# A maximum over partitions by two products of TensorE, placed behind the values, in a decode kernel with attention and a gated feed-forward

## The chip, the core and the metric

The kernel runs on one core of a Trainium2 chip. A core has five engines that run side by side and wait for each other by semaphores: TensorE (PE in the profile; its loads of the stationary operand are listed as PEld), VectorE (DVE), ScalarE (ACT), GpSimd (POOL) and SyncE (SP), which issues most of the transfers. The transfers themselves are done by 16 DMA engines, which bring data from HBM to the on-chip memory SBUF. TensorE writes its results to PSUM, a second on-chip memory in banks of 512 values per partition. The metric is the device time of one execution in microseconds (us).

## What is computed

One token is decoded. `g * attention(x) + (1 - g) * feed_forward(x)`, with `g` a sigmoid of a product of `x` and `gate_w`.

```python
# B, Sq, D = 1, 1, 512;  Hq, Hkv, Sk, Dh = 32, 8, 32768, 128;  F = 1792;  all float32
def _A_ref(x, k_cache, v_cache, wq, wo):
    q = (x @ wq).reshape(B, Sq, Hq, Dh).transpose(0, 2, 1, 3)
    k = jnp.repeat(k_cache, rep, axis=1)          # rep = 4 query heads on each head of the cache
    v = jnp.repeat(v_cache, rep, axis=1)
    scores = jnp.einsum("bhqd,bhkd->bhqk", q, k) * (Dh ** -0.5)
    p = softmax(scores, axis=-1)
    o = jnp.einsum("bhqk,bhkd->bhqd", p, v)
    return o.transpose(0, 2, 1, 3).reshape(B, Sq, Hq * Dh) @ wo

def _B_ref(x, w1, w3, w2):
    return (silu(x @ w1) * (x @ w3)) @ w2

g = sigmoid((x * gate_w).sum(-1, keepdims=True))
return g * _A_ref(...) + (1 - g) * _B_ref(...)
```

The caches of keys and of values are 134 MB each, and every byte is read once. The softmax needs, for each of the 32 query heads, the largest of 32768 scores before the exponentials.

## The kernel before

**Units.** The eight heads of the cache are taken in pairs. A pair's keys come in four units of 8 MB, so there are 16 units of keys (`t` = 0 to 15), and its values in four units of 8 MB (`v`). Values run `LAG` = 4 units behind keys: unit `v` of values is multiplied in the pass of unit `t = v + 4` of keys. Units of keys alternate with units of values in the queue of SP. Two large buffers, `big_a` and `big_b`, take them: keys go to `big_a` (the units 0 and 2 to `big_b`), values to `big_b`. A buffer is loaded again once what reads it is done.

**One pass.** When a unit of keys has landed, ACT sets part of its second half aside (`set_aside`, L318), and DVE transposes it in eight steps (`scores`, L346), two halves `z` of four `c`. Each step gives PE its operand for the scores (L330), added up in one PSUM bank. ACT copies the scores out (L358) and later copies the weights of the values (`weights`, L420, written to `pv`). PE multiplies the unit of values (`values_all`, L432), 32 products, and then a product with zeros (L242) clears the bank of the scores. The next load of keys waits for L318 and for the scores of the second half; the next load of values (L413) waits for L432.

**The softmax.** After each fourth unit (`t` = 3, 7, 11, 15) PE turns the scores of the pair by 16 transpositions into four PSUM banks named `turned` (`turn`, L368), so that 128 positions lie on the partitions and each partition holds 2048 values: 256 positions by 8 heads. DVE then takes the maximum over the 256 (L379, tile `mt`, 128 partitions by 8 heads). The maximum over the 128 partitions follows in eleven small instructions of DVE: a transposition of 32 by 32 blocks (L381), four reductions (L383), one more (L385), four copies that spread it (L388) and a second transposition (L390). Then DVE subtracts it in place (L391), ACT takes the exponentials to `probs` (L398), and DVE sums them in a later pass (L405).

**Order.** The order on every engine is written out by hand. A recorder (`Program.add`) works out the waits from what each step reads and writes; `credits` are semaphores that a PE step waits for and takes down again, as PE runs its passes as real loops: one of 4 passes without values, one of 12 with values. In the second loop the turning stands under a counter, so that it runs in each fourth pass, ahead of the values. Each loop's first instruction is laid on a code block's edge. `columns`, `hidden_products` (L463, the two products of the feed-forward with w1 and w3, once, behind unit 3) and everything behind the second loop are straight-line code. L463 writes the PSUM banks `pm[0]` and `pm[1]` (`ps` in the profile) and reads w1 and w3 from `big_b`; the first load of values waits for it.

**The end.** Behind the loop come the last two heads' values (L587), the products with wo (L574, L660) and with w2 (L676), and the store. Transfers of 8 MB, 4 MB and at last 3.5 MB in five pieces bring their operands. The first load into `big_a` behind the loop is multiplied by L587 and is followed there by another load, which waits for it.

## Time and profile before

| what | value |
|---|---|
| median of 3 runs | 694.13 us (693.95 to 694.29) |
| the profiled execution | 693.89 us, its span 692.1 us |
| bytes read from HBM | 296.23 MB, 428 GB/s over the span |
| busy: PE, DVE, ACT | 388.3, 370.1 and 134.7 us |
| share of the 16 DMA engines taken by the loads | 99.1% |
| granted clock of TensorE, mean | 0.802 |

The span goes from the first to the last instruction of the program. The page of the profile gives busy times by engine, a picture of the span in 40 slices, the DMA queues, the chain of work that ended last, and groups of instructions by line. The order of time lists instructions as "start, duration, engine, line, operation, out<-in, count [idle time before it <- what ended it]". A window's row lists the stretch, its length, the busy time and the count of instructions of PE, PEld, DVE, ACT and POOL, the granted clock, the share of the DMA engines and GB/s. The waits of SP are the time in which a load was not yet issued; a load that is issued also queues behind those issued before it.

### The profile page before, as it was taken

What the parts mean: (1) busy time and instruction counts of PE and PEld (TensorE: products, weight loads), DVE (VectorE), ACT (ScalarE), POOL (GpSimd) and SP (SyncE); (2) the same over time, 40 slices, a digit from 0 to 9 for tenths busy, and PEclk for the clock granted to TensorE, in tenths of its full rate; (3) what the DMA queues carried; (4) which work ended last, traced back from release to release, by engine and by line L of the source; (5) the groups of instructions that cost most, each with busy time, mean ns of one, the idle gap of its engine ahead of it and who ended that gap; (6) DMA issues with size and microseconds to landing.
All of it is one profiled execution on the core that took longest, in us unless ns stands there. A gap on an engine that the chain in (4) does not pass through costs nothing. (4 is left out here: it accounts for less than half of the span.)

```text
span 692.1 us, 5789 instructions
## 1 busy us (share of the span) xinstructions
PE 388.3 (56%) x2448; PEld 95.3 (14%) x2448; DVE 370.1 (53%) x259; ACT 134.7 (19%) x113; POOL 2.8 (0%) x15
## 2 busy tenths in 40 slices
PE   1537677566473636565564646364563646564457
PEld 0101111201010101201010101101010101211112
DVE  1049998493725637493826537492816547600701
ACT  0143323222303131220303131220303031100000
POOL 1000000000000000000000000000000000000000
PEclk9969999968686966778695779788697879865789
DMA  9999999999999999999999999999999999999996
GB/s 394 444 432 424 428 424 432 449 439 432 424 432 424 443 447 432 428 428 428 432 443 443 428 428 428 428 443 447 432 424 428 428 436 439 421 451 425 422 429 287
DMA packets 6213, 296.35 MB, mean 428 GB/s; under 512 B 694, under 2 KB 698, under 8 KB 1084
## 3 DMA queue, kind: packets, MB, share of 16 engines
q1 hardware_dynamic: 6196, 296.23, 99.1%
q8 instruction: 6, 0.10, 0.1%
q14 instruction: 3, 0.02, 0.0%
q10 hardware_dynamic: 8, 0.01, 0.0%
HBM read 296.23 MB, written 0.00 MB: 428 GB/s over the span
## 5 line engine op out<-in xcount | busy, mean ns | idle before, releaser
L346 DVE STREAM_TRANSPOSE aside<-big_a 128x2048 f32<-128x2048 f32 x41 | 94.4, 2302 | 184.3 <-DMA big_a<-in_A_k_cache_dram 184.3
L330 PE MATMUL ps<-aside,winc 128*32 128x512 f32 x512 | 89.4, 776 | 168.0 <-PEq L703 167.2
L330 PE MATMUL ps<-kt,winc 128*32 128x512 f32 x512 | 89.0, 772 | 49.1 <-PEq L703 49.1
L318 ACT COPY aside<-big_a 128x6144 f32<-128x6144 f32 x14 | 74.4, 5313 | 171.2 <-DMA big_a<-in_A_k_cache_dram 171.2
L432 PE MATMUL ps<-big_b,pv 128*32 128x512 f32 x768 | 94.9, 650 | 17.4 <-PEq L703 17.4
L346 DVE STREAM_TRANSPOSE kt<-aside 128x2048 f32<-128x2048 f32 x32 | 72.7, 2273 | 0.0
L346 DVE STREAM_TRANSPOSE kt<-big_a 128x2048 f32<-128x2048 f32 x28 | 63.5, 2269 | 0.0
L330 PEld LDWEIGHTS ps<-aside,winc 128*32 128x32 f32 x512 | 13.1, 120 | 236.6 <-issue 236.6
L358 ACT COPY sb<-ps 128x512 f32<-128x512 f32 x16 | 17.1, 1071 | 136.5 <-PE ps L330 136.5
L432 PEld LDWEIGHTS ps<-big_b,pv 128*32 128x32 f32 x768 | 27.7, 119 | 85.0 <-issue 85.0
L346 DVE STREAM_TRANSPOSE aside<-aside 128x2048 f32<-128x2048 f32 x16 | 36.3, 2269 | 0.0
L587 PE MATMUL ps<-big_b,probs 128*32 128x512 f32 x128 | 19.1, 756 | 21.1 <-DMA big_b<-in_A_v_cache_dram 21.1
L330 PEld LDWEIGHTS ps<-kt,winc 128*32 128x32 f32 x512 | 13.1, 120 | 125.4 <-issue 125.4
L596 DVE TENSOR_SCALAR red<-ps,own_b 128x128 f32<-128x128 f32 x2 | 0.7, 350 | 52.7 <-PE ps L587 52.7
L324 ACT COPY winc<-win 128x128 f32<-128x128 f32 x32 | 9.8, 307 | 77.9 <-PE ps L330 77.9
L587 PE MATMUL ps<-big_a,probs 128*32 128x512 f32 x128 | 18.1, 730 | 7.6 <-DMA big_a<-in_A_v_cache_dram 7.6
L346 DVE STREAM_TRANSPOSE aside<-big_b 128x2048 f32<-128x2048 f32 x7 | 16.0, 2291 | 11.0 <-DMA big_b<-in_A_k_cache_dram 11.0
L641 PE MATMUL ps<-win,ones 128*128 128x512 f32 (+1 forms) x40 | 21.8, 631 | 0.0
L242 PE MATMUL ps<-acc 128*128 128x512 f32 x34 | 20.0, 670 | 2.5 <-POOL acc L213 1.5
L379 DVE TENSOR_REDUCE mt<-turned 128x8 f32<-128x2048 f32 x4 | 9.2, 2292 | 20.3 <-PE turned L368 20.3
L405 DVE TENSOR_REDUCE sums<-probs 128x8 f32<-128x2048 f32 x4 | 15.3, 3834 | 2.1 <-ACT probs L398 2.1
L268 PE MATMUL turned<-big_a,xp 128*32 128x512 f32 x64 | 8.6, 699 | 12.0 <-DMA big_a<-in_A_wq_dram 12.0
(94 smaller groups left out, 186.9 us busy)
## 6 DMA issues: line engine op xcount, KB each, us to landing
big_b<-in_A_v_cache_dram SPq DMA_DIRECT2D x2, 4096.0 KB, 25.8
big_b<-in_B_w_dram SPq DMA_DIRECT2D x2, 3584.0 KB, 20.8
aside<-in_A_wo_dram SPq DMA_DIRECT2D x1, 4096.0 KB, 29.4
big_a<-in_A_wo_dram SPq DMA_DIRECT2D x1, 4096.0 KB, 20.4
big_a<-in_B_w_dram SPq DMA_DIRECT2D x2, 1024.0 KB, 23.5
big_a<-in_B_w_dram SPq DMA_DIRECT2D x1, 768.0 KB, 26.0
big_a<-in_B_w_dram SPq DMA_DIRECT2D x1, 512.0 KB, 26.7
big_a<-in_B_w_dram SPq DMA_DIRECT2D x1, 256.0 KB, 26.9
```

The lines of the kernel that those rows point to most:

```text
L242: return T.matmul(ps_s, acc[:, 0:P], acc, start=True, stop=False, skip_group_check=True)
L268: ins = T.matmul(pf[b][32 * j:32 * j + 32, :], xp[:, c, :], t[:, o:o + REP * DH], start=(c == 0), stop=(c == NC - 1),)
L318: act(lambda: A.copy(spare, src[:, :, 32:128]), reads=[key], writes=["wo"])
L324: lambda: A.copy(winc, win[:, t // 4, :, 16 - 16 * z:48 - 16 * z]),
L330: ins = T.matmul(ps_s[32 * g:32 * g + 32, :], winc[:, c, :], kt[c % 2][:, 512 * g:512 * g + 512], start=False, stop=False, skip_group_chec ...
L346: k = dve(lambda d=dst, s=src: V.transpose(d, s), reads=[key], writes=[f"kt{c % 2}"], credit="keys")
L358: lambda: A.copy(sb[:, :, :, t % 4], ps_s.rearrange("p (n i) -> p n i", i=32)),
L379: dve(lambda: V.tensor_reduce(mt[:, 0:8], turned.rearrange("p (n q) -> p q n", q=8), axis=AX.X, op=ALU.max), reads=banks, writes=["mt"])
L405: dve(lambda: V.tensor_reduce(sums[:, 8 * w:8 * w + 8].rearrange("p (u q) -> p u q", u=2), probs[:, :, 0:1024].rearrange("p u (n q) -> p u ...
L432: ins = T.matmul(ps_o[32 * t:32 * t + 32, :], pv[:, o:o + 32], big[1][:, n * P:(n + 4) * P], start=((z, g) == (0, 0)), stop=((z, g) == (1, ...
L587: ins = T.matmul(ps_o[32 * t:32 * t + 32, :], prob[u][:, o:o + 32], vt[:, n * P:(n + 4) * P], start=((e, z, g) == (0, 0, 0)), stop=((e, z, ...
L641: return T.matmul(bank[:, 0:n], ones, win.rearrange("p w c n -> p (w c n)")[:, 0:n], start=True, stop=True)
```

## The change

The maximum over the 128 partitions is done by two products of TensorE. One transposes `mt`, 128 partitions by 8, into 8 partitions by 128 in `pm[0]`; DVE reduces that to `high`, one value on each of 8 partitions, and multiplies the 8 by 8 corner of the unit matrix by it (`diag`). A product of ones (8 by 128) with `diag` then puts all 8 maxima on each of 128 partitions in `pm[1]`, and DVE copies them to `top`. These two products and the steps between them stand right behind the turning in PE's order. In the second loop the turning and the maximum stand behind the values instead of ahead of them; a new semaphore, `maxima`, tells PE when `mt` and when `diag` is written. In unit 3 both products stand ahead of L463. One clearing of `mt` by POOL goes. And DVE's program is preceded by a directive that lays its first instruction on an edge of 128 instructions, with a jump over the padding.

```diff
-    mt, mtt, mark, mark2 = sbuf("mt", 32), sbuf("mtt", 32), sbuf("mark", 1), sbuf("mark2", 1)
-    quads, high, wide_t, top = sbuf("quads", 4), sbuf("high", 1), sbuf("wide_t", 32), sbuf("top", 32)
+    mt, mark, mark2 = sbuf("mt", 8), sbuf("mark", 1), sbuf("mark2", 1)
+    high, diag, top = sbuf("high", 1), sbuf("diag", 8), sbuf("top", 8)
...
+    def maxima(w, loop):
+        banks = [f"f{f}" for f in range(4)]
+        most, spread = pm[0][0:8, 0:P], pm[1][:, 0:8]
+        m = dve(lambda: V.tensor_reduce(mt, turned.rearrange("p (n q) -> p q n", q=8), axis=AX.X, op=ALU.max),
+                reads=banks, writes=["mt"], credit="maxima" if loop else None)
+        pe(max_turn, reads=["mt", "ident"], writes=["m0"], loop=loop, credits=((m, 1),) if loop else ())
+        dve(lambda: V.tensor_reduce(high[0:8, :], most, axis=AX.X, op=ALU.max), reads=["m0"], writes=["high"])
+        d = dve(lambda: V.tensor_scalar(diag[0:8, :], ident[0:8, 0:8], high[0:8, 0:1], None, op0=ALU.mult),
+                reads=["high", "ident"], writes=["diag"], credit="maxima" if loop else None)
+        pe(max_spread, reads=["ones", "diag"], writes=["m1"], loop=loop, credits=((d, 1),) if loop else ())
+        dve(lambda: V.tensor_copy(top, spread), reads=["m1"], writes=["top"])
+
+    def max_turn():
+        return T.transpose(pm[0][0:8, 0:P], mt, ident)
+
+    def max_spread():
+        return T.matmul(pm[1][:, 0:8], ones[0:8, :], diag[0:8, :], start=True, stop=True)
 
     def softmax(w):
         banks = [f"f{f}" for f in range(4)]
-
-        dve(lambda: V.tensor_reduce(mt[:, 0:8], turned.rearrange("p (n q) -> p q n", q=8), axis=AX.X, op=ALU.max),
-            reads=banks, writes=["mt"])
-        dve(lambda: V.transpose(mtt, mt), reads=["mt"], writes=["mtt"])
-        for k in range(4):
-            dve(lambda k=k: V.tensor_reduce(quads[0:32, k:k + 1], mtt[32 * k:32 * k + 32, :], axis=AX.X, op=ALU.max),
-                reads=["mtt"], writes=[("quads", k)])
-        dve(lambda: V.tensor_reduce(high[0:32, :], quads[0:32, :], axis=AX.X, op=ALU.max),
-            reads=[("quads", k) for k in range(4)], writes=["high"])
-        for k in range(4):
-            dve(lambda k=k: V.tensor_copy(wide_t[32 * k:32 * k + 32, :], high[0:32, :].to_broadcast([32, 32])),
-                reads=["high"], writes=[("wide_t", k)])
-        dve(lambda: V.transpose(top, wide_t), reads=[("wide_t", k) for k in range(4)], writes=["top"])
         dve(lambda: V.tensor_tensor(
             turned.rearrange("p (n q) -> p n q", q=8), turned.rearrange("p (n q) -> p n q", q=8),
-            top[:, 0:8].unsqueeze(1).to_broadcast([P, 256, 8]), op=ALU.subtract,
+            top.unsqueeze(1).to_broadcast([P, 256, 8]), op=ALU.subtract,
         ), reads=["top"], writes=banks)
...
         if v >= 1:
             own(v - 1)
+        if v >= 0:
+            values_loop(vals.pop(v), weights(v), out_op)
         if t % 4 == 3:
-            turn(v >= 0, out_op if v >= 0 else ())
+            turn(v >= 0)
+            maxima(t // 4, v >= 0)
         if v >= 0:
-            values_loop(vals.pop(v), weights(v), () if t % 4 == 3 else out_op)
             clear(loop=True)
...
+    V.addr_align(128, offset=0, max_nops=0)
     for e in ("SP", "ACT", "DVE", "POOL"):
         pr.emit(e)
...
         unit()
+        take("values", 16)
+        take("weights")
+        values_all().then_inc(done, 1)
         T.reg_sub(left, left, 1)
         with T.If_cmp(left, 0, "IS_EQ"):
             for f in range(4):
                 turn_part(f).then_inc(done, 1)
+            for part in (max_turn, max_spread):
+                take("maxima")
+                part().then_inc(done, 1)
             T.reg_mov(left, 4)
-        take("values", 16)
-        take("weights")
-        values_all().then_inc(done, 1)
         zeros().then_inc(done, 1)
```

More of the change, by code (lines that the diff above doesn't have):

```diff
@@ L220 @@
     for n, t in (
-        ("win0", win), ("otp", otp), ("mt", mt), ("pvpad", pv[:, 512:528]), ("pad0", prob[0][:, 1024:1040]), ("pad1", prob[1][:, 1024:1040])
+        ("win0", win), ("otp", otp), ("pvpad", pv[:, 512:528]), ("pad0", prob[0][:, 1024:1040]), ("pad1", prob[1][:, 1024:1040])
     ):
@@ L369, in turn_part, with turn @@
         return ins
-    def turn(loop, credits=()):
+    def turn(loop):
         for f in range(4):
-            pe(lambda f=f: turn_part(f), reads=[("sb", m) for m in range(4)] + ["ident"], writes=[f"f{f}"], loop=loop,
-               credits=credits if f == 0 else ())
+            pe(lambda f=f: turn_part(f), reads=[("sb", m) for m in range(4)] + ["ident"], writes=[f"f{f}"], loop=loop)
+    def maxima(w, loop):
[9 more added lines that the diff above has]
+        dve(lambda: V.tensor_copy(top, spread), reads=["m1"], writes=["top"])
```

## The prediction

> **What bounds the kernel now.** I read the profile's page first (busy shares, slices, queues, chain), then the DMA issues' landing times, then the order of time around the four maxima.

> ```profile
> span 692.1 us, 5789 instructions
> ...
> PE 388.3 (56%) x2448; PEld 95.3 (14%) x2448; DVE 370.1 (53%) x259; ACT 134.7 (19%) x113; POOL 2.8 (0%) x15
> ...
> DMA  9999999999999999999999999999999999999996
> ...
> q1 hardware_dynamic: 6196, 296.23, 99.1%
> q8 instruction: 6, 0.10, 0.1%
> q14 instruction: 3, 0.02, 0.0%
> HBM read 296.23 MB, written 0.00 MB: 428 GB/s over the span
> ```

> No engine is busy for more than 56% of the span; the 16 DMA engines are busy for 99.1% of it with q1, and only the last of 40 slices shows less than 9. So the transfer is the bound: what the change does to PE and DVE counts only where it leaves the DMA engines without work, or where it comes after the last byte.

> ```profile
> 0.90:1.90 1.00, 0.36 (x1) 0.36 (x2) 0.00 (x0) 0.12 (x1) 0.81 (x3) 1.00 0.01 2
> 1.90:2.90 1.00, 1.00 (x2) 0.14 (x1) 0.53 (x3) 1.00 (x1) 0.90 (x3) 1.00 3.12 1049
> ...
> 661.57 26.71 DMA big_a<-in_B_w_dram
> ```

> Two windows of the profile (the last two columns are DMA share and GB/s) and a row of the chain. The first load is issued 0.9 us into the span and bytes flow from 1.9: an issue needs about 1.0 us before its bytes move. The last load has landed at 661.57 + 26.71 = 688.28. That leaves 1.9 us ahead of the stream and 692.1 - 688.28 = 3.8 us behind it, 5.7 us together, and q1's missing 0.9% is 6.2 us. So inside the stream about half a microsecond is idle, over all: there is nearly nothing to win there.

> **How much room the loads have.** A load hides its issue as long as it is queued before the one ahead of it has landed.

> ```profile
> DMA to landing us min/median/max: 26.0/28.5/30.0
> ```

> This is the answer for the loop's loads of values (L413), 8 MB each. At the 428 GB/s of the page's mean, 8.39 MB take 19.6 us, so every such load has waited in the queue for 6.4 to 10.4 us. An issue may come some 5.4 us later (6.4 less the 1.0 above) before any engine runs dry.

> **The change part by part.** *The small steps of the maximum.* Eleven instructions of DVE go per stage (L381, four L383, L385, four L388, L390) and three come, with a transposition and a product on PE between them: 4 x 8 = 32 of the 259 fewer.

> ```profile
> 124.32 6.22 PE L463 MATMUL ps<-big_b,xp 128*32 128x448 f32 x64
> 124.43 2.29 DVE L379 TENSOR_REDUCE mt<-turned 128x8 f32<-128x2048 f32 x1 [5.36 <-PE turned L368]
> ...
> 129.06 2.30 DVE L391 TENSOR_TENSOR turned<-turned,top 128x2048 f32<-128x2048 f32 x1
> 130.60 0.33 SPq L413 DMA_DIRECT2D big_b<-in_A_v_cache_dram  x1
> ...
> 137.91 2.31 DVE L346 STREAM_TRANSPOSE aside<-big_a 128x2048 f32<-128x2048 f32 x1 [6.55 <-DMA big_a<-in_A_k_cache_dram]
> ```

> Before, from the end of L379 (126.72) to the start of L391 it is 2.34 us. The new chain has no rows of its own, so nearest ones:

> ```profile
> L602 PEld LDWEIGHTS ps<-own_q,red x4: 186/188/189, 643.1 to 678.0; 128*128 128x128 f32 x4
> L602 PE MATMUL ps<-own_q,red x4: 253/263/273, 643.1 to 678.0; 128*128 128x4 f32 x4
> L568 DVE TENSOR_REDUCE otp<-each x2: 284/286/287, 608.7 to 679.7; 128x16 f32<-128x128 f32 x1, 64x16 f32<-64x128 f32 x1
> L281 DVE TENSOR_SCALAR gate<-gate x1: 154/154/154, 32.2 to 32.2; 128x1 f32<-128x1 f32 x1
> L259 DVE COPY xp<-ps x1: 165/165/165, 11.0 to 11.0; 128x4 f32<-128x4 f32 x1
> ```

> Each PE step about 0.4 us (a load and its pass, partly doubled), the reduction over 128 0.29, the diagonal 0.15, the copy out of PSUM 0.17: 1.4 us, and 0.1 for each of the four hand-overs, 1.8 us. Bounds: 1.4 without hand-overs, and at half clock of PE with 0.2 for each hand-over 3.0. I take 1.8: DVE's part gets about 0.5 us shorter. Off the path, so nothing.

> *Unit 3, the tightest place.* There are no values yet, and the two maxima products stand ahead of the hidden products L463, which also write the banks that DVE now reads. L463 began at 124.32, with the turning just done; now it waits for L379 and the chain, 126.72 + 1.8 - 0.3 (only its first bank is needed at first) = 128.2, and ends at 134.4 instead of 130.54. Behind it hangs the first load of values, issued at 130.60, now at 134.5. Its bytes can move from 135.5; the keys ahead of it land at 137.91. Hidden, with 2.4 us to spare. Without that cover it would cost the whole 3.9 us.

> What eats the spare is PE's clock.

> ```profile
> 130.60:135.40 4.80, 0.00 (x0) 0.00 (x0) 0.76 (x1) 3.22 (x3) 0.00 (x0) 1.00 1.03 440
> 135.50:137.90 2.40, 0.00 (x0) 0.00 (x0) 0.00 (x0) 0.00 (x0) 0.00 (x0) 0.50 1.03 440
> 286.06:289.00 2.94, 0.99 (x2) 0.16 (x2) 0.00 (x0) 2.93 (x3) 0.00 (x0) 1.00 0.98 424
> 289.10:292.70 3.60, 0.00 (x0) 0.00 (x0) 0.00 (x0) 0.18 (x1) 0.00 (x0) 0.50 0.80 346
> ...
> 546.12 9.89 PE L432 MATMUL ps<-big_b,pv 128*32 128x512 f32 x64 [1.95 <-PEq L703]
> ```

> In these windows the third column from the right is the granted clock. It was halved 4.9 us after PE's last work in one place (130.54 to 135.4) and 2.0 us after it in another (286.06 + 0.99 = 287.05, to 289.1). The new gap, 124.4 to 128.2 with two small products in it, lies between. If it halves, the nearest price is L432 at 9.89 us against the 7.07 it takes at full clock (row below): up to 2.8 us more. L463 would then end between 134.4 and 137.2, its load's bytes flow between 135.5 and 138.3: the stream loses 0 to 0.4 us. Where the half clock lasts for all of L463 (12.4 us, end at 140.6, bytes at 141.7), it loses 3.8 us. I take 0, the value that holds until L463 is 2.4 us late, and keep 3.8 as the far end.

> [...]

> *Units 7 and 11: values before the turning.* Unit 7 is the tighter, as ACT loads a table there.

> ```profile
> 275.42 3.58 PE L368 MATMUL turned<-ident,sb 128*128 128x128 f32 x16 [1.53 <-PEq L703]
> ...
> 278.92 7.07 PE L432 MATMUL ps<-big_b,pv 128*32 128x512 f32 x64
> ...
> 286.05 1.28 ACT L398 ACT_TABLE_LOAD   x1 [10.34 <-DVE turned L391]
> 286.06 0.33 SPq L413 DMA_DIRECT2D big_b<-in_A_v_cache_dram  x1
> 287.34 1.94 ACT L398 ACTIVATE probs<-turned 128x1024 f32<-128x1024 f32 x2
> ...
> 292.71 5.31 ACT L318 COPY aside<-big_a 128x6144 f32<-128x6144 f32 x1 [3.44 <-DMA big_a<-in_A_k_cache_dram]
> ...
> L346 DVE STREAM_TRANSPOSE kt<-big_a 128x2048 f32<-128x2048 f32 x28 | 63.5, 2269 | 0.0
> ```

> Values start about 275.7 (pv is copied just then), half of it at half clock: 8.6 us, end 284.3, so the load that waits for them is issued 1.8 us earlier: hidden already, worth 0. Then turning 2.0 (286.3), L379 2.3 (288.6), the chain 1.8 (290.4), the subtraction 2.3 (292.7), table and exponentials 1.3 + 1.9 (295.9). The next keys land at 292.71. DVE is free just then; ACT starts L318 3.2 us late and ends at 301.2. Who waits for that: DVE's sixth transposition of the unit, five of about 2.2 us after 292.71, at 303.8. So 2.6 us are left; then the load of keys behind both has its own lead. PE, held in `take("maxima")`, delays only the clearing product and then waits for keys anyway. With values at 9.89 and the turning at 3.58 everything is 2.9 us later; keys would be freed up to 3 us late, within the 5.4 us above. Cost 0, bound 0.5.

> *The last maximum.* Here it lies on the listed chain, and it is moved behind 7.07 us of values.

> ```profile
> 584.40 1.97 PE turned L368 x16
> ...
> 608.33 9.52 PE ps L587 x64
> 617.85 0.02 issue
> 617.87 33.18 DMA big_a<-in_A_v_cache_dram
> ```

> The chain takes 7.07 less 0.5 = 6.6 us more, so L587 ends at 624.4 and the load into the first buffer is issued there, not at 617.87. It needs 33.18 us to land where 19.6 are its own: 13.6 us of queue, less 6.6 and 1.0, leave 6.0. Even at half clock for all of L587 (14.1 us, +4.6) it holds. What follows 631.7 is set by landings, as before. Cost 0.

> *DVE's code.* The q14 row has 3 blocks in 0.02 MB, under 8.4 KB each, and under 0.05% of 16 engines' span, so below 1.8 us each on one engine; q8's six hold 17 KB each. A block that is fetched delays one of 16 engines, and a landing needs all. One or two of DVE's fewer: between nothing and 0.6 us, or as much lost when one falls on an engine that is late already; I take -0.2. The jump over padding at the start falls on DVE before its first wait for data (xp is written at 11.0, L259); several microseconds fit there: 0. [...]

> **Sum.** On the profiled execution, 693.89 us (span 692.1 and 1.8 around it): 0 + 0 + 0 - 0.2 = 693.7. The median of the runs is 694.13, 0.24 above that, so 693.9.

> **The rivals.** (a) *Slower: the first load of values starves the stream.* Place: unit 3, L463 at half clock and later by the chain. It begins to count when L463 ends after 136.9, and exceeds 0.2% (1.4 us, about what a measurement here tells from no change) from 138.3. For it: the gap of 3.8 us. Against: 2.4 us of cover, and half clock seldom lasts. Time 695.4 to 697.9. [...] (c) *Faster: code fetches cost more than their packets.* The idle half microsecond within the stream and 0.6 for fetches bound it: 692.8. (d) *It does less than it says*: fetches stay as many; 694.1, inside no change.

> **How the numbers follow.** No change with (d) 0.80; (a) beyond 0.2% 0.10; (b) beyond it 0.04; (c) beyond it 0.06. Faster 0.06, same 0.80, slower 0.14. The range, 692.8 to 695.9, goes from (c) to the lower part of (a).

> **What would show it.** L463 begins near 128.2 and the load behind it is issued near 134.5, its keys still landing at 137.9; L318 of unit 8 starts near 296, the last L587 of buffer A ends near 624, DVE has 227 instructions, the DMA slices still read 9 and the last load lands within 1 us of 688.3. Wrong, if a DMA slice near 138 us dips or the queue rows for code grow.

## The result

The changed kernel is slower by 0.3%: 695.97 us (median of 8 runs, 695.35 to 697.54) against 694.08 us before (8 runs, 693.91 to 694.29); the ratio is 1.0031 with a 95% interval of 1.002 to 1.0042. The forecast was 693.9 us and no change. What came was rival (a), the starved stream behind unit 3, and the time lies inside the 695.4 to 697.9 us that was given for it; by which rule it got there is another matter (see "Why the prediction was wrong"). The profiled execution took 696.57 us.

The page of the changed kernel:

```profile
span 694.2 us, 5786 instructions
...
PE 399.0 (57%) x2460; PEld 99.0 (14%) x2460; DVE 365.0 (53%) x227; ACT 134.4 (19%) x113; POOL 2.7 (0%) x14
...
DMA  9999999999999999999999999999999999999996
GB/s 401 439 427 427 423 431 453 386 420 427 434 461 430 423 427 427 446 453 420 427 427 434 453 434 423 427 427 438 457 427 427 423 430 446 420 449 428 422 423 282
...
q1 hardware_dynamic: 6196, 296.23, 98.9%
q8 instruction: 5, 0.08, 0.0%
q14 instruction: 4, 0.03, 0.0%
HBM read 296.23 MB, written 0.00 MB: 427 GB/s over the span
```

The span is 2.1 us longer and the loads' share is 98.9% instead of 99.1%. The busy digits of the DMA row still read 9 up to the last slice; the loss shows in the row under it. The eighth slice of 17.35 us, 121.5 to 138.8, moved 386 GB/s, the lowest value before the last slice. DVE has 227 instructions, as forecast. The queue of DVE's code, q14, has one block more than before (4, not 3), though the code became shorter. Both signs that the prediction named for being wrong have come: a dip near 138 us, in GB/s, and a grown row of code.

The order of time in unit 3 of the changed kernel:

```profile
122.53 1.91 PE L368 MATMUL turned<-ident,sb 128*128 128x128 f32 x16
124.47 2.29 DVE L378 TENSOR_REDUCE mt<-turned 128x8 f32<-128x2048 f32 x1 [5.36 <-PE turned L368]
...
126.82 0.27 PE L388 MATMUL ps<-ident,mt 128*8 128x128 f32 x1 [2.39 <-DVE mt L378]
127.14 0.28 DVE L381 TENSOR_REDUCE high<-ps 8x1 f32<-8x128 f32 x1 [0.37 <-PE ps L388]
127.45 0.22 DVE L382 TENSOR_SCALAR diag<-ident,high 8x8 f32<-8x8 f32 x1
127.72 0.38 PE L391 MATMUL ps<-diag,ones 8*128 8x8 f32 x2 [0.63 <-DVE diag L382]
128.04 7.92 PE L467 MATMUL ps<-big_b,xp 128*32 128x448 f32 x64
128.14 0.17 DVE L385 COPY top<-ps 128x8 f32<-128x8 f32 x1 [0.48 <-PE ps L391]
128.34 2.30 DVE L395 TENSOR_TENSOR turned<-turned,top 128x2048 f32<-128x2048 f32 x1
...
136.01 0.33 SPq L417 DMA_DIRECT2D big_b<-in_A_v_cache_dram  x1
...
137.75 2.31 DVE L346 STREAM_TRANSPOSE aside<-big_a 128x2048 f32<-128x2048 f32 x1 [7.10 <-DMA big_a<-in_A_k_cache_dram]
...
178.60 2.31 DVE L346 STREAM_TRANSPOSE aside<-big_a 128x2048 f32<-128x2048 f32 x1 [15.51 <-DMA big_a<-in_A_k_cache_dram]
...
565.62 2.31 DVE L346 STREAM_TRANSPOSE aside<-big_a 128x2048 f32<-128x2048 f32 x1 [18.43 <-DMA big_a<-in_A_k_cache_dram]
```

The chain of the maximum runs as described. The hidden products (L463 before, L467 now) start at 128.04 and take 7.92 us. The load of values behind them (L413 before, L417 now) is issued at 136.01; before it was issued at 130.60. The last three rows are the first transposition of units 4, 5 and 15, which start as their keys land. Here are the two later ones before:

```profile
176.61 2.31 DVE L346 STREAM_TRANSPOSE aside<-big_a 128x2048 f32<-128x2048 f32 x1 [12.88 <-DMA big_a<-in_A_k_cache_dram]
...
563.93 2.31 DVE L346 STREAM_TRANSPOSE aside<-big_a 128x2048 f32<-128x2048 f32 x1 [18.43 <-DMA big_a<-in_A_k_cache_dram]
```

Unit 4's keys land as before (137.75 against 137.91). Unit 5's are 1.99 us late, unit 15's 1.69. The load that the chain lists last lands at 690.37 (below) against 688.28, 2.1 us late. So the loss arises between the keys of units 4 and 5, where only the first load of values lies, and is carried to the end.

The chain of the changed kernel, its last part:

```profile
619.12 9.59 PE ps L593 x64
628.71 0.02 issue
628.73 24.01 DMA big_a<-in_A_v_cache_dram
...
664.46 25.91 DMA big_a<-in_B_w_dram
```

Windows of before and then of the changed kernel, around the gap. The columns are the stretch, its length, the five engines, the granted clock, the DMA share and GB/s. A packet seems to be booked where it begins, as shares above 1 occur (1.23 and 2.14 here), so a low share means that few packets began.

```profile
135.00:136.00 1.00, 0.00 (x0) 0.00 (x0) 0.00 (x0) 0.00 (x0) 0.00 (x0) 0.71 1.23 533
136.00:137.00 1.00, 0.00 (x0) 0.00 (x0) 0.00 (x0) 0.00 (x0) 0.00 (x0) 0.50 0.93 393
137.00:138.00 1.00, 0.00 (x0) 0.00 (x0) 0.09 (x1) 0.09 (x1) 0.00 (x0) 0.50 0.46 197
```

```profile
135.00:136.00 1.00, 0.95 (x12) 0.13 (x4) 0.00 (x0) 0.00 (x0) 0.00 (x0) 1.00 0.02 8
136.00:137.00 1.00, 0.00 (x0) 0.00 (x0) 0.00 (x0) 0.00 (x0) 0.00 (x0) 1.00 0.99 328
137.00:138.00 1.00, 0.00 (x0) 0.00 (x0) 0.26 (x1) 0.26 (x1) 0.00 (x0) 1.00 2.14 721
```

Between 135 and 136 almost nothing began (8 GB/s), though the keys ahead land only at 137.75. The trace's records of single packets say why. The 16 DMA engines didn't finish this load together: from 135.56 the first of them had no packet of q1 left, and until 137.76 an engine stood idle for 1.25 us on average. Before, it was 0.02 us.

### The profile page after: what moved, and what is told of

Same layout as the page of the kernel before. It is cut to its first block, busy times and chain, and to the rows that moved or that the text cites. A ratio compares the mean times of both kernels' runs of the same rounds, so it can differ in the third digit from the quotient of the medians.

```text
span 694.2 us, 5786 instructions
## 1 busy us (share of the span) xinstructions
PE 399.0 (57%) x2460; PEld 99.0 (14%) x2460; DVE 365.0 (53%) x227; ACT 134.4 (19%) x113; POOL 2.7 (0%) x14
## 2 busy tenths in 40 slices
DMA  9999999999999999999999999999999999999996
## 3 DMA queue, kind: packets, MB, share of 16 engines
q1 hardware_dynamic: 6196, 296.23, 98.9%
HBM read 296.23 MB, written 0.00 MB: 427 GB/s over the span
## 5 line engine op out<-in xcount | busy, mean ns | idle before, releaser
L346 DVE STREAM_TRANSPOSE aside<-big_a 128x2048 f32<-128x2048 f32 x41 | 94.4, 2302 | 175.2 <-DMA big_a<-in_A_k_cache_dram 175.2
L330 PE MATMUL ps<-aside,winc 128*32 128x512 f32 x512 | 93.1, 806 | 157.1 <-PEq L710 156.3
L330 PE MATMUL ps<-kt,winc 128*32 128x512 f32 x512 | 91.8, 796 | 45.1 <-PEq L710 45.1
L318 ACT COPY aside<-big_a 128x6144 f32<-128x6144 f32 x14 | 74.4, 5313 | 160.6 <-DMA big_a<-in_A_k_cache_dram 160.6
L436 PE MATMUL ps<-big_b,pv 128*32 128x512 f32 x768 | 92.1, 634 | 22.9 <-PEq L710 22.9
L346 DVE STREAM_TRANSPOSE kt<-aside 128x2048 f32<-128x2048 f32 x32 | 72.7, 2273 | 0.0
L346 DVE STREAM_TRANSPOSE kt<-big_a 128x2048 f32<-128x2048 f32 x28 | 63.5, 2269 | 0.0
L436 PEld LDWEIGHTS ps<-big_b,pv 128*32 128x32 f32 x768 | 29.1, 116 | 92.0 <-issue 92.0
L346 DVE STREAM_TRANSPOSE aside<-aside 128x2048 f32<-128x2048 f32 x16 | 36.3, 2269 | 0.0
L242 PE MATMUL ps<-acc 128*128 128x512 f32 x34 | 22.8, 756 | 2.5 <-POOL acc L213 1.5
L602 DVE TENSOR_SCALAR red<-ps,own_b 128x128 f32<-128x128 f32 x2 | 0.7, 350 | 43.3 <-PE ps L593 43.3
L346 DVE STREAM_TRANSPOSE aside<-big_b 128x2048 f32<-128x2048 f32 x7 | 16.1, 2298 | 10.6 <-DMA big_b<-in_A_k_cache_dram 10.5
## 6 DMA issues: line engine op xcount, KB each, us to landing
aside<-in_A_wo_dram SPq DMA_DIRECT2D x1, 4096.0 KB, 28.5
big_a<-in_A_wo_dram SPq DMA_DIRECT2D x1, 4096.0 KB, 19.6
```

The costliest lines, as they stand in the source:

```text
L242: return T.matmul(ps_s, acc[:, 0:P], acc, start=True, stop=False, skip_group_check=True)
L318: act(lambda: A.copy(spare, src[:, :, 32:128]), reads=[key], writes=["wo"])
L330: ins = T.matmul(ps_s[32 * g:32 * g + 32, :], winc[:, c, :], kt[c % 2][:, 512 * g:512 * g + 512], start=False, stop=False, skip_group_chec ...
L346: k = dve(lambda d=dst, s=src: V.transpose(d, s), reads=[key], writes=[f"kt{c % 2}"], credit="keys")
L436: ins = T.matmul(ps_o[32 * t:32 * t + 32, :], pv[:, o:o + 32], big[1][:, n * P:(n + 4) * P], start=((z, g) == (0, 0)), stop=((z, g) == (1, ...
```

## The experiments

All were timed in five rounds against the kernel before on the same chip; whose median there was 694.04 to 694.19 us. The products and reductions that some kernels add are idle, their results unused; no kernel leaves work out.

**1. Hidden products first.** The changed kernel, with L463's work ahead of the maximum again. Unit 3's two small products write the bank of the values, as `pm` is in use.

```diff
         if t % 4 == 3:
             turn(v >= 0)
+            if t == LAG - 1:
+                hidden_products()
             maxima(t // 4, v >= 0)      # in unit 3 to ps_o instead of pm[0], pm[1]
...
-        if t == LAG - 1:
-            hidden_products()
```

> The changed kernel, but in unit 3 the hidden products (L467) stand ahead of the maximum again, whose two products use the bank of the values, free by then. Theory T1 (all of the loss is the first load of values, issued 5.4 us later in unit 3, after the keys' engines have begun to run dry): the load is issued near 130.6 us again, unit 5 of keys lands near 176.6 and the time is that of the kernel before, 694.1 (693.6 to 694.5). T2 (the loss comes from the later stages, the values ahead of the turning, or from code blocks): the time stays at 695.5 to 696.5.

Measured: 694.98 us, ratio 1.0012 (1.0003 to 1.0021). The load is issued at 130.76 again and the keys land as before (unit 15 at 563.84). So about 1.0 us of the loss went away with the late load, and some 0.8 us is left that has another source: experiments 8 and 9.

**2. Only unit 3's maximum.** The kernel before with the two small products in unit 3 alone, ahead of the hidden products. The order of the loop, the three other maxima and DVE's start stay.

```diff
         if t % 4 == 3:
             turn(v >= 0, out_op if v >= 0 else ())
+        if t == LAG - 1:
+            maxima()                    # softmax(0) then starts at the subtraction
```

> The kernel before, with the maximum by two products of TensorE in unit 3 alone, ahead of the hidden products; the three other stages, the order in the loop and the code's place as before. T1: the whole loss is there, 695.9 (695.2 to 697), with executions that differ by up to 2 us. T2: 694.1, as before.

Measured: 696.33 us, 1.0039 (1.0025 to 1.0052). Its order of time:

```profile
128.46 7.73 PE L477 MATMUL ps<-big_b,xp 128*32 128x448 f32 x64
...
136.26 0.33 SPq L427 DMA_DIRECT2D big_b<-in_A_v_cache_dram  x1
```

Unit 3 alone costs what the whole change costs, within the intervals.

**3. PE kept busy.** The changed kernel with two idle products between unit 3's turning and its maximum, so that PE's gap is filled.

```diff
             turn(v >= 0)
+            if v < 0:
+                for _ in range(2):
+                    pe(lambda: T.matmul(ps_o, ones, <512 values of win>), reads=["ones"], writes=["o"])
             maxima(t // 4, v >= 0)
```

> The changed kernel, with two idle products (512 columns each) behind unit 3's turning, which keep PE at work while it waits for the first maximum. T1 with the half clock as its decisive part: L467 runs at full clock, 6.2 us, the load is issued near 134.3 to 134.5 and bytes flow at 135.4, before or just as the engines run dry: 694.1 to 694.6. T1 without it (the order alone does the harm): 695.5 or more. T2: 695.5 to 696.5.

Measured: 696.08 us, 1.0033 (1.0023 to 1.0043).

```profile
128.21 6.22 PE L467 MATMUL ps<-big_b,xp 128*32 128x448 f32 x64
...
134.49 0.33 SPq L417 DMA_DIRECT2D big_b<-in_A_v_cache_dram  x1
```

The hidden products took 6.22 us, as in the kernel before, and the load was issued at 134.49, exactly where the prediction had it for the full clock, and the kernel was still slow. So the half clock alone isn't what decides: an issue at 134.5, called hidden "with 2.4 us to spare", is already too late. (This kernel also fetches two more blocks of PE's code, 7 on q8 instead of 5, one of them at 135.8 us, inside the gap. The execution profiled in experiment 5 has none there; its L467 took 6.22 us too, the load was issued at 134.51, and unit 5's keys came 0.59 us late. That is less than the 1.99 us of the changed kernel, so the half clock isn't free either.)

**4. The order alone.** The kernel before with the turning behind the values in the loop, as in the change, and nothing else.

```diff
+        take("values", 16)
+        take("weights")
+        values_all().then_inc(done, 1)
         T.reg_sub(left, left, 1)
         with T.If_cmp(left, 0, "IS_EQ"):
             ...
-        take("values", 16)
-        take("weights")
-        values_all().then_inc(done, 1)
```

> The kernel before, with the values ahead of the turning in the second loop, and nothing else of the change: DVE's eleven instructions, unit 3 and the code's place as before. T1: nothing is lost, 694.1 (693.7 to 694.5). T2, where the moved order is the cause: 695.5 to 696.5.

Measured: 694.12 us, 1.0000 (0.9991 to 1.0009). The new place of the turning in units 7, 11 and 15 is free. (This kernel keeps DVE's eleven instructions; experiment 8 has the new maximum there as well.)

**5. The changed kernel without the directive.**

```diff
-    V.addr_align(128, offset=0, max_nops=0)
     for e in ("SP", "ACT", "DVE", "POOL"):
         pr.emit(e)
```

> The changed kernel without the directive that lays DVE's program on an edge. T1: 696.0 (695.3 to 697.5), the same as with it. If the code blocks were part of the loss: nearer to 694.1. If the directive wins what was forecast for it, this run is 0.2 us slower than the changed kernel, which the spread of the executions will hide.

Measured: 695.87 us, 1.0026 (1.0017 to 1.0036), which this can't tell from the changed kernel's 1.0031. The directive isn't what makes the changed kernel slow.

**6 and 7. The load of values held back in the kernel before, by PE.** Four and six idle products behind the hidden products also read the buffer, so the load waits for them.

```diff
             pe(ff, reads=[f"B{z}", "xp"], writes=[f"m{z}"])
+        for _ in range(4):              # 6 in the other kernel
+            pe(lambda: T.matmul(ps_o, ones, <512 values of win>),
+               reads=["ones", "B0", "B1"], writes=["o"])
```

> The kernel before; behind the hidden products stand four idle products of 512 columns that the first load of values waits for as well. PE stays at full clock, so the load is issued near 130.6 + 3.8 = 134.4 us instead of 130.6. T1: bytes flow from 135.4, the engines run dry from about 135.6: 694.1 (to 694.4). A rule that any lateness counts would give 697.9.

> As the run with four idle products, with six: the load is issued near 136.3 us. T1: this is as late as in the changed kernel's profile (136.01), so about the same loss, 1.9 to 2.4 us: 696.0 to 696.5. By the forecast's rule (only what comes after the keys' landing at 137.9, less 1.0, counts) 694.1. T2: 694.1.

Measured: issued at 134.27, 695.61 us, 1.0021 (1.0012 to 1.003); issued at 135.96, 695.83 us, 1.0027 (1.0018 to 1.0037). The kernel before, with only that load held back to where the changed kernel issues it (135.96 against 136.01), loses nearly as much. The added products bring code of their own, but experiment 11 loses 1.2 us with no product added. Together with experiment 1 that shows the late issue as the cause. The expected 694.1 to 694.4 for four products was missed, so here an issue needed more lead than the 1.0 us that T1 gave it.

**8 and 9. The directive where the load isn't late.** Experiment 1 without the directive, and the kernel before with the directive alone.

```diff
-    V.addr_align(128, offset=0, max_nops=0)     # experiment 8: taken out of experiment 1
```

```diff
+    V.addr_align(128, offset=0, max_nops=0)     # experiment 9: put into the kernel before
```

> The run with the hidden products first, without the directive on DVE's place. That run kept 0.8 us; its keys landed as in the kernel before up to 563.8 us, and its last load 0.85 us later. Theory D (the rest is a block of DVE's code, which the directive brings to the tail near 654 us, where it holds one DMA engine up): 694.1 (693.8 to 694.4). Theory M (the rest is the maximum on PE or PE's later code): 695.0 as with it.

> The kernel before with the directive alone (DVE's program keeps its length). D: one block of code more is fetched and its edges lie elsewhere, with no effect or up to 0.8 us more, by where the fetch falls: 694.1 to 694.9. M: 694.1.

Measured: 694.04 us, 0.9996 (0.9987 to 1.0005), and 694.93 us, 1.0008 (0.9999 to 1.0018; its 11 runs 694.57 to 695.81). Removing it from experiment 1 gains 0.94 us (694.98 less 694.04); adding it to the kernel before costs 0.76 (694.93 less 694.17). The interval of each run by itself includes no change, but both ways round agree, and the spans lie apart: 692.9 to 693.3 us with the directive against 692.0 to 692.3 without (experiments 1 and 8), 692.8 to 693.2 with it against 692.0 to 692.4 (experiment 9 and the kernel before, with one of its 32 runs at 692.9). The code queue and the chain of the kernel with the directive (experiment 1) and then of that without it (experiment 8):

```profile
q14 instruction: 4, 0.03, 0.0%
...
662.56 26.58 DMA big_a<-in_B_w_dram
```

```profile
q14 instruction: 3, 0.02, 0.0%
...
662.57 25.59 DMA big_a<-in_B_w_dram
```

The load that the chain lists last is issued alike and lands 1.0 us later. The packet records of the code queue have blocks at 5.1, 140.4, 315.7 and 654.1 us with the directive and at 114.2, 138.1 and 509.1 without: moved to that edge, DVE's program needs one block more.

The landings show what such a block did. A load's landing is counted in 16 steps, each some 0.5 us behind the last packet that a DMA engine has of the load (unit 4's keys in the changed kernel: last packets at 135.55 to 137.22, steps at 136.05 to 137.72). Of the load that is under way at 654.1, 15 steps come 9.71 us behind those of the load ahead of it, and one comes 0.97 us later than that. That engine stayed behind to the end. The first product that waits for this load, with the directive and then without:

```profile
661.65 0.16 PEld L594 LDWEIGHTS ps<-big_b,probs 128*32 128x32 f32 x8 [1.88 <-DMA big_b<-in_A_v_cache_dram]
```

```profile
660.67 0.16 PEld L594 LDWEIGHTS ps<-big_b,probs 128*32 128x32 f32 x8 [0.88 <-DMA big_b<-in_A_v_cache_dram]
```

In experiment 9 the blocks come at 5.2, 135.8, 272.1 and 608.1, none near 654; there the last of the 16 steps fell back by 0.96 us in the load under way at 608.1, and stayed behind. So two kernels with the fetch at two places show the same. The other blocks in these traces agree: from 160 us to the end of the stream, each block of DVE's code put the engines back by some 0.9 to 1.1 us in sum (0.65 once), each block of PE's by 1.4 to 1.7, and where single steps can be told apart it was one engine that bore it. The landing was late only by what this engine then lay behind the last of the others: for the block at 429.4 of the kernel before, 0.3 us.

**10 to 13. Where the room ends.** The kernel before, its first load of values held back by other engines, with no more code on PE: behind the first or the second exponential of unit 3, or behind one or two idle reductions of DVE.

```diff
-            "SP", lambda: nc.sync.dma_start(big[1], vd[s // 2, s % 2]), writes=["B0", "B1"], over=["extra"],
+            ... over=["extra", *([LATE] if s == 0 else [])],   # LATE: ("prob", 0), ("prob", 1) or "late"
...
             softmax(t // 4)
+        if v + 1 == 0:
+            for _ in range(n):          # only with "late": n = 1 or 2
+                dve(lambda: V.tensor_reduce(red[5][:, 0:1], <768 values of win>), writes=["late"], ...)
+            vals[0] = load_values(0)
```

> The kernel before; the first load of values also waits for the first exponentials of unit 3 (their end is 133.7 us), with no instruction added on PE. By the forecast's rule (bytes must flow by the keys' landing, 137.9) 694.1. By T1 (engines begin to run dry from about 135.6, an issue needs 1.0 us): 694.1 to 694.4. If a load must be queued much earlier than that: 695 or more.

> As the run that waits for the first exponentials, with the second (134.7 us). By the forecast's rule 694.1. T1: bytes at 135.7, just as the first engines run dry: 694.2 to 695.0. If the run of six idle products (issue at 135.96, 1.8 us lost) owed its loss to lateness and not to its added PE code, this one lies between 694.1 and 695.8.

> The kernel before; the first load of values also waits for one added reduction of DVE over 768 columns, behind unit 3's subtraction (131.4 us), some 0.85 us long: the load is issued near 132.3 instead of 130.6, 3.3 us ahead of the first engine that runs dry. The runs so far: no loss at 130.6, 1.3 us at 134.15. If a lead of some 2 us suffices: 694.1. If it doesn't: 694.6 or more.

> As the run with one added reduction, with two: the load is issued near 133.1 us, 2.5 us ahead of the first engine that runs dry. If a lead of some 2 us suffices: 694.1. If the loss grows evenly from 130.6 to 134.15 (1.3 us): 695.0.

The rows of the issue with one reduction, with two, behind the first exponential and behind the second, one fence for each kernel:

```profile
132.35 0.33 SPq L413 DMA_DIRECT2D big_b<-in_A_v_cache_dram  x1
```

```profile
133.41 0.33 SPq L413 DMA_DIRECT2D big_b<-in_A_v_cache_dram  x1
```

```profile
134.15 0.33 SPq L413 DMA_DIRECT2D big_b<-in_A_v_cache_dram  x1
```

```profile
134.94 0.33 SPq L413 DMA_DIRECT2D big_b<-in_A_v_cache_dram  x1
```

The kernels that hold that load back, and the kernel before, in the order of their issue ("none seen" is 0.02 us, the same as before; "no directive" is experiment 5, "unit 3 only" experiment 2). The idle time of a DMA engine (mean of the 16) between 135.5 and 138.4, from the packet records, and the landing of unit 5's keys are of the profiled execution; medians and ratios are of all runs.

| kernel | issued | engine idle near 137, us | unit 5's keys land | median, us | ratio (95%) |
|---|---|---|---|---|---|
| before | 130.60 | none seen | 176.61 | 694.08 | 1 |
| one reduction | 132.35 | none seen | 176.53 | 694.17 | 1.0000 (0.9991 to 1.0009) |
| two reductions | 133.41 | none seen | 176.58 | 694.34 | 1.0003 (0.9994 to 1.0012) |
| first exponential | 134.15 | 0.13 | 176.77 | 695.46 | 1.0018 (1.0009 to 1.0027) |
| four products | 134.27 | 0.28 | 176.81 | 695.61 | 1.0021 (1.0012 to 1.003) |
| PE kept busy | 134.49 | 0.65 | 178.03 | 696.08 | 1.0033 (1.0023 to 1.0043) |
| no directive | 134.51 | 0.47 | 177.20 | 695.87 | 1.0026 (1.0017 to 1.0036) |
| second exponential | 134.94 | 0.63 | 178.24 | 695.35 | 1.0014 (1.0005 to 1.0023) |
| six products | 135.96 | 1.06 | 177.63 | 695.83 | 1.0027 (1.0018 to 1.0037) |
| changed kernel | 136.01 | 1.25 | 178.60 | 695.97 | 1.0031 (1.002 to 1.0042) |
| unit 3 only | 136.26 | 1.52 | 178.50 | 696.33 | 1.0039 (1.0025 to 1.0052) |

Up to 133.4 no cost is seen (the intervals end at 0.6 and 0.8 us); from 134.15 the median is 1.2 us higher and more. The idle time of the engines grows with the issue, by and large, but the median doesn't grow in step: it rises by 1.2 to 1.3 us at once and then slowly to about 2. The times expected for the two exponentials by T1 (up to 694.4 and 695.0) were missed, as with four products. Runs of one kernel spread more behind the step (694.39 to 697.05 in 11 runs behind the first exponential, 693.78 to 695.16 in 32 of the kernel before on that chip).

The step isn't the price at the gap. The column of unit 5's keys has that price: 0.2 us for the first exponential and for four products, 0.6 to 2.0 us from 134.49 on. More was lost later, where a block of code met the engine that ended last. Unit 12's keys of the kernel before, and of the one behind the first exponential:

```profile
447.82 2.31 DVE L346 STREAM_TRANSPOSE aside<-big_a 128x2048 f32<-128x2048 f32 x1 [9.54 <-DMA big_a<-in_A_k_cache_dram]
```

```profile
448.58 2.31 DVE L346 STREAM_TRANSPOSE aside<-big_a 128x2048 f32<-128x2048 f32 x1 [9.51 <-DMA big_a<-in_A_k_cache_dram]
```

Unit 8's keys were 0.17 us late in that execution, unit 12's are 0.76, although the kernel before loses 0.3 us of its own there: in the load under way at 427.8, when a block of DVE's code is fetched, the last engine fell 0.9 us further behind the first. With four products the same happened at the block of PE's code of 597.2, by 1.35 us, and with the second exponential at that of 675.8, by 1.2. In the kernel before none of its blocks cost more than 0.3. So a late load may cost more by changing which engine ends last; that it does so in most executions, and thus makes the step of the medians, isn't shown, as one execution of each kernel was profiled.

## Why the prediction was wrong

**The step that failed** is in the part on the room of the loads: "An issue may come some 5.4 us later before any engine runs dry", and with it, for unit 3, "Its bytes can move from 135.5; the keys ahead of it land at 137.91. Hidden, with 2.4 us to spare." The room was between 2.8 and 3.6 us, not 5.4: issued at 133.41 instead of 130.60 the load costs nothing that is seen, at 134.15 it does. Two sizes in it were wrong. The landing of a load was taken as the moment at which the queue runs dry. The landing counted the slowest of the 16 engines: the first had nothing left at 135.56 (135.54 to 135.72 in the seven runs with a gap), 2.2 us before the keys landed. Of these, 1.7 us lie between the first engine's last packet of keys and the last engine's (137.22), and 0.5 between that and the landing. And the 1.0 us from issue to bytes, read from the idle start, was that of the first engine and too short as a lead for all. In the changed kernel the first bytes moved 0.95 us after the issue, as forecast. But the engines got theirs one after another: the last engine that had to wait got its first packet 2.6 us after an issue at 133.41, 2.7 after 134.15, 2.9 after 134.27 and 3.5 after 134.49 (matched by their times, as the records don't name the engine). So an issue at 134.27, 1.45 us ahead of the first idle time in its run (135.72), already left five engines idle. The rival's point "when L463 ends after 136.9" should have lain between 133.4 and 134.1, and full clock alone was then enough to reach it (L463 to 134.4).

**The price behind that point** was taken as the lateness itself. It wasn't. In the changed kernel the engines idle for 1.25 us on average, and their first packets behind the gap take 3.12 us on average instead of 2.45 before; the two make 1.9 us, and the next keys land 1.99 us late. (Such a sum fits less well elsewhere: 1.7 us with six products, where they land 1.02 late.) And just past the point, where the gap itself costs 0.2 us, the median is 1.2 us higher; the text behind the table has what is known of that.

**Unit 3's own times** were right. L467 starts at 128.04 (forecast 128.2); the small steps take 1.58 us (126.76 to 128.34; forecast 1.8), and the four hand-overs between DVE and PE in them 0.04 to 0.06 us each, not the 0.1 that the forecast put in without a row for it.

**PE's clock.** L467 at 7.92 us against 6.22 ends at 135.96, inside 134.4 to 137.2. The granted clock was 0.50 from 129.3 to 132.7 us, 3.4 us that began 1.2 us into L467 and cost it half of that. That is the difference of 1.70 us. So the range held; what failed is the 0 that the forecast took for it, on the 2.4 us of cover. And the kernel with PE kept busy shows that the time was no better with L467 at 6.22 us. (That "half clock seldom lasts" has this ground: the twelve passes of L432 took 7.07 to 9.89 us in the kernel before, none the 14.1 of half clock throughout.)

**Units 7 and 11, and the last maximum:** right, shown by the order alone (1.0000) and with the new maximum by experiment 8 (0.9996). L318 of unit 8 began at 295.41 (forecast 296). The product out of the first load behind the loop ended at 628.71 (forecast 624.4: the keys came 1.7 us later, and the values ahead of the turning waited 1.1 us for their weights and took 8.48 us instead of 7.07). The load behind it took 24.01 us to land; with the prediction's 19.6 us for its own bytes, it still queued for over 4 us.

**DVE's code:** -0.2 was wrong in sign. The 32 instructions fewer came as forecast, but the edge made one block more, not fewer; alone it costs 0.76 to 0.94 us. The prediction's far end for it was 0.6 lost, "when one falls on an engine that is late already": that is what experiments 1 and 9 show, and the size was too small. No run shows the gain of 0.2 that the sum had. In the changed kernel the directive's removal can't be told from nothing: the two losses didn't add up. In its profiled execution the block at 656.5 put the landings back by 0.4 us only, as it fell on an engine that was some 0.6 us ahead of the last.

**Rivals.** (b), with its 0.04, was that PE's loop fetches code in each of its twelve passes. It didn't: the page has five blocks on q8 for the whole span, against six before. (c) and (d) fell with the result. (a) got 0.10 on the ground of its 2.4 us of cover; that cover was not there. That the time lies in (a)'s range is luck: L467 ended at 135.96, ahead of its 136.9, so by its own rule nothing would have been lost.

**A reading.** The load that lands at 688.28 isn't the last: the piece issued behind it, at 662.04, lands at 688.9. By the prediction's own sum that leaves 5.1 us outside the stream and about 1.1 us idle within, not half a microsecond. Only the bound of rival (c) rests on it.

## What to carry to other kernels

On a stream that is full, measure the room of a load to the moment at which the first DMA engine has run dry, not to the landing that the waiting instruction shows: here the two lay 2.2 us apart (135.56 and 137.75), and an issue 2.1 us before the first showed no cost (133.41), one 1.4 us before it did (134.15). So look for the one load with the least lead when a step is moved ahead of what frees its buffer, and hold that load back in the old kernel to price the delay by itself. Count code blocks by a run after a directive that moves a program's start: here 32 instructions fewer came with one block more (4 on q14, not 3), and in experiment 1 the block at 654.1 us put one engine back by 0.97 us, and the last load landed 1.0 us later than in experiment 8.
